# Attention of the third token block spread over five row tiles, its inputs loaded earlier, its decays on GpSimd

## The chip, the cores and the metric

One core of a Trainium2 chip runs the whole program. The metric is the device time of one execution in microseconds (us), as the median of several runs; the profile is one execution of its own, with its own time.

## The reference

Three layers follow one another, all in float32 precision. First a retention (linear attention with decay) over batch 4, 8 heads, 768 positions, head size 64. Then an ELU layer from 512 to 2048 and back, and a "maxout" layer with three 512 x 768 matrices and a last 768 x 512 matrix, on 3072 tokens.

```python
for t in range(S):                        # retention, for each batch and head
    state = gamma * state + outer(k[t], v[t])
    y[t] = scale * q[t] @ state
h = x @ w_in                              # ELU layer
x = where(h > 0, h, exp(min(h, 0)) - 1) @ w_out
h = maximum(maximum(x @ w1, x @ w2), x @ w3)
return h @ w_out2
```

The moe weights are float64 numbers, which the kernel turns into float32 pairs (high and low part) itself.

## The kernel before

**Chunks, blocks, steps.** The 3072 tokens are 24 chunks `c` of 128 tokens (6 to a batch) and 6 blocks `b` of 512 tokens (4 chunks each). Retention is done by chunk: `scores` multiplies k and q (16 small matmuls, L153), `mask` multiplies them by the decay mask on VectorE (L165), `prep` makes the decayed `qd` (L129) and `kd` (L137), `update` adds this chunk to the running state (PE L181, VectorE L188 and L191), `mix` multiplies state and `qd` (L204) and the masked scores and v (L208), and copies the result to `xh` on ScalarE (L216); `rest` makes its low part `xl` on VectorE (L221). `begin(c)` is scores, prep and mask; `end(c)` is update and mix. A block's ELU layer runs over 16 row tiles `f` of the hidden layer: `h1(b, f)` is 12 matmuls (L338), then exp, relu, max, and a split into high part `gh` (ScalarE, L348) and low part `gl` (VectorE, L351); `o1(b, f)` is 12 matmuls (L370) that add to four accumulators in PSUM.

**Order.** `seq` (L492 and below) lists pairs (b, f). Blocks 0 and 1 take turns while their weights are still being converted; they fill steps i = 0 to 31, blocks 2 to 5 follow from step 32 (`split`). Step i of the main loop (L767) issues h1 of entry i+1 and then o1 of entry i. The orders of SyncE's DMA queue, TensorE, VectorE and ScalarE are the order of the program text; GpSimd's is the scheduler's. Steps 26 to 29 are (1, 12) to (1, 15), steps 30 and 31 are (0, 14) and (0, 15), and step 32 is (2, 0). Step 26's o1 begins at 207.66 us of the profile, step 32's at 271.95 us. Chunks 8 to 11 (`EARLY` is 8) are block 2, so their attention has to be done before h1(2, 0), which step 31 issues; chunk 12 begins block 3. In steps 28 to 31 the kernel does this:

```python
if i == split - 6: load(c)                        # c = 8
if i == split - 4: prep(c); scores(c, ...); mask(c)
if i == split - 3: load(c + 1); new_x(2); end(c); rest(c); prep(c + 1)
if i == split - 2: load(c + 2); scores(c + 1, ...); mask(c + 1); end(c + 1)
                   load(c + 3); begin(c + 2); rest(c + 1)
if i == split - 1: o1(b, f, f0, f1); end(c + 2); begin(c + 3); load(c + 4); rest(c + 2)
                   end(c + 3); rest(c + 3); begin(c + 4); x2_out(...); h1(*seq[i + 1][:2])
```

From block 3 on, `values` and `following` spread one chunk over four steps. `x2_out` closes a group of steps: VectorE adds the accumulators to a partial sum, four instructions (L387), and SyncE writes the sums out where the block is done.

**Buffers.** A chunk of block 0 or 1 lies in a slot of `wpool` (13 slots of 8 KB per partition, tag `w`), a later one in `ld` (2 slots, tag `r`, shared with the partial sums of x2_out). A load from chunk 8 on is five DMAs: four of 128 KB (L98), one of 512 KB (L106). A slot of `wpool` otherwise holds the converted weights of one f below 13; those of f = 9 to 12 are written to DRAM (`keep`, `kept`) and fetched again into `ring` (3 slots for each of two halves) for blocks 2 and up (`fetch`, L416). `qd`, `kd` and `a` have one buffer each; odd chunks below 8 use a `spare` slot of `wpool` in their place. Scores, updates, mixes and h1 share the four PSUM buffers of `ps_h`. `xh` and `xl` have two buffers each, which blocks 0 and 1 hold until the h1 of their f = 15, in steps 28 and 30. In steps up to 27 VectorE converts one half of an f per step (L279 to L306) from `raw`, which `load_half` (L243) has SyncE load two halves ahead.

Of the kernel before, what the change touches and what calls it, by code (L numbers as in the profile page):

```python
# [7 lines left out]
F32 = mybir.dt.float32  # L8
# [7 lines left out]
B, H, S, D = 4, 8, 768, 64  # L16
P = 128
# [13 lines left out]
RES = 9  # L31
# [9 lines left out]
def kernel(ctx: ExitStack, tc: tile.TileContext, qkv0, qkv, wa, wb, dmask, qdec, cols, out):  # L41
# [18 lines left out]

    dmask_sb = const.tile([P, H, P], F32, name="dmask_sb")
    qdec_sb = const.tile([P, NPAIR, P], F32, name="qdec_sb")
    cols_sb = const.tile([P, H + NPAIR], F32, name="cols_sb")
    state = [const.tile([P, NPAIR, D], F32, name=f"state{i}") for i in range(2)]
    x2d = dram.tile([KDM, P, NT], F32, name="x2d")
    kept = {(f, c): dram.tile([P, 2 * 512], F32, name=f"kept{f}_{c}") for f in range(RES, KFF) for c in range(2)}
# [11 lines left out]
    def load(c, part=None):  # L78


        if c >= NCHUNK:
            return

        early = c < EARLY
        src = qkv0 if early else qkv
        if part != 1:
            if c in raw_t:
                return
            if early:
                x = wpool.tile([P, NPAIR, 4, P], F32, tag="w", name="x")  # L90
            else:
                x = ld.tile([P, NPAIR, 4, P], F32, tag="r", name="x")
            raw_t[c] = x
            for r in range(2):
                h = slice(r * D, (r + 1) * D)
                for s in range(1 if early else 2):
                    cc = slice(s * 2 * P + r * P, s * 2 * P + (r + 1) * P)
                    nc.sync.dma_start(out=x[h, :, s, :], in_=src[c, :, h, cc].rearrange("p d t -> d p t"))  # L98
            if early:
                nc.sync.dma_start(  # L100
                    out=x[:, :, 1, :], in_=src[c, :, :, 2 * P:3 * P].rearrange("p t n -> t p n")
                )
        if part != 0:
            x = raw_t[c]
            o = 3 * P if early else 4 * P
            nc.sync.dma_start(  # L106
                out=x[:, :, 2:4, :].rearrange("t p s n -> t p (s n)"),
                in_=src[c, :, :, o:].rearrange("p t n -> t p n"),
            )
# [3 lines left out]
    def prep(c):  # L113

        if c >= NCHUNK:
            return
        x = raw_t[c]
        early, pool = c < EARLY, nc.vector if c <= EARLY + CB else nc.gpsimd
        if early and c % 2:
            if not spare:  # L120
                spare.append(wpool.tile([P, 4, NPAIR, P], F32, tag="w", name="spare"))
            sp = spare[0]
            qd, kd, a = sp[:, 0], sp[:, 1].rearrange("t p (r d) -> t p r d", r=2), sp[:, 2:4]
        else:
            qd = at.tile([P, NPAIR, P], F32, tag="qd", name="qd") if c % NCH != 0 else None
            kd = at.tile([P, NPAIR, 2, D], F32, tag="kd", name="kd") if c % NCH != NCH - 1 else None
            a = None
        if c % NCH != 0:
            pool.tensor_tensor(out=qd, in0=x[:, :, 0, :], in1=qdec_sb, op=ALU.mult)  # L129
        kt = x[:, :, 2, :].rearrange("t p (r d) -> t p r d", r=2)  # L130
        if c % NCH == NCH - 1:
            pass
        elif early:
            for h in range(H):
                nc.scalar.activation(kd[:, h // 2, h % 2], kt[:, h // 2, h % 2], ACTF.Copy, scale=cols_sb[:, h:h + 1])
        else:
            pool.tensor_tensor(  # L137
                out=kd, in0=kt,
                in1=cols_sb[:, 0:H].rearrange("t (p r) -> t p r", r=2).unsqueeze(3).to_broadcast([P, NPAIR, 2, D]),
                op=ALU.mult,  # L140
            )
        st_t[c] = (qd, kd, a)

    def scores(c, pool, tag):

        if c >= NCHUNK:
            return
        x = raw_t[c]
        sc = sc_t[c] = [pool.tile([P, NPAIR, P], F32, tag=tag, name="sc") for _ in range(2)]
        for p in range(NPAIR):  # L150
            for r in range(2):
                h = slice(r * D, (r + 1) * D)
                nc.tensor.matmul(sc[r][:, p, :], x[h, p, 1, :], x[h, p, 0, :], start=p == 0, stop=p == NPAIR - 1)  # L153

    def mask(c):
        if c >= NCHUNK:
            return
        sc = sc_t.pop(c)
        a = st_t[c][2]
        if a is None:  # L160
            a = at.tile([P, 2, NPAIR, P], F32, tag="a", name="a")
        else:
            a = a.rearrange("t r p i -> t r p i")
        for r in range(2):
            nc.vector.tensor_tensor(  # L165
                out=a[:, r], in0=sc[r], in1=dmask_sb.rearrange("j (p r) i -> j r p i", r=2)[:, r], op=ALU.mult
            )
        a_t[c] = a
# [358 lines left out]
    def begin(c, pool=ps_h, tag="h"):  # L527
        scores(c, pool, tag)
        prep(c)
        mask(c)  # L530

    def end(c):
        update(c, ps_h, "h")
        mix(c, ps_h, "h")
# [232 lines left out]
    for i, (b, f, f0, f1) in enumerate(seq):  # L767
        if i < 2:
            continue
        if (b, f0) in units:  # L770
            done = (units[b, f0] - 1) * CB + f // CB
            if f % CB == 1:
                values(done)
            elif f % CB == 2:
                following(done)
        c = EARLY
        if i == split - 6:
            load(c)
        if i == split - 4:
            prep(c)  # L780
            scores(c, ps_h, "h")
            mask(c)
        if i == split - 1:
            part_t[b] = []
            for m in range(KDM):
                o = f32(dpool.tile([P, BLK], (I32, F32)[m % 2], tag="tm"[m % 2], name="tm"[m % 2]))
                nc.sync.dma_start(out=o, in_=x2d[m, :, b * BLK:(b + 1) * BLK])
                part_t[b].append(o)
            o1(b, f, f0, f1)
            end(c + 2)  # L790
            begin(c + 3)
            load(c + 4)
            rest(c + 2)
            end(c + 3)
            rest(c + 3)
            begin(c + 4)
            x2_out(b, f0, f1, False)
            h1(*seq[i + 1][:2])
            continue
        if i == len(seq) - 5:  # L800
            pump(100000)
            reopen()
            load_sums(0)
            sums(0)
            for k in XORD:
                later.append(lambda k=k: split_sum(0, k))
        if i == len(seq) - 4:
            fetch_set(loads[-1][0])
        if i == len(seq) - 3:
            fetch_set(loads[-1][1])  # L810
            fetch_set(loads[-1][2])
        if i + 1 == len(seq):
            break
        if i < split and n < 2 * KFF:
            h1(*seq[i + 1][:2], [(cv_high, n)], [(cv_bits, n + 1)] if n + 1 < 2 * KFF else [])
        elif i >= len(seq) - 5:
            h1(*seq[i + 1][:2], [], [(catch_up, 1)])
        elif i > split:
            h1(*seq[i + 1][:2], [(pump, 2)], [(pump, 2)])
        else:  # L820
            h1(*seq[i + 1][:2])
        o1(b, f, f0, f1)
        if f == f1 - 1:
            x2_out(b, f0, f1, f1 < KFF and (b, f0) != (0, 10))
        if i >= len(seq) - 5:
            catch_up(2)
        elif i > split:
            pump(1 if b < NB - 1 and f % CB in (1, 2) else 4)
        if i == split - 3:
            load(c + 1)  # L830
            new_x(2)
            end(c)
            rest(c)
            prep(c + 1)
        if i == split - 2:
            load(c + 2)
            scores(c + 1, ps_h, "h")
            mask(c + 1)
            end(c + 1)
            load(c + 3)  # L840
            begin(c + 2)
            rest(c + 1)
        if i < split and n < 2 * KFF:
            cv_low(n)
            if n + 1 < 2 * KFF:
                cv_rest(n + 1)
            n += 1
            if i == 2:
                cv_high(n)
                cv_bits(n + 1)  # L850
                cv_low(n)
                cv_rest(n + 1)
                n += 1
        while i < split and done_f < n // 2:
            if done_f >= RES:
                keep(done_f)
            done_f += 1
        for c, g in ((0, i + 1), (1, i)):
            if g < len(seq):
                b, f = seq[g][:2]  # L860
                if f >= KFF - NRING and (b + 1 < NB if b >= 2 else (b, f) in ((1, 13), (0, 14), (0, 15)) and g > 24):
                    fetch(RES + f - (KFF - NRING), c)
                if b >= 2 and RES <= f < KFF - NRING:
                    fetch(f + NRING, c)
    catch_up(99)
# [105 lines left out]
```

## Time and profile before

| | |
|---|---|
| median of 3 runs | 1034.04 us (1031.86 to 1034.31) |
| profiled execution: its time, its span | 1032.82 us, 1030.7 us |
| busy: TensorE, VectorE, ScalarE, GpSimd | 98%, 67%, 34%, 2% of the span |
| granted TensorE clock, mean | 0.989 |

The span runs from the first to the last instruction; the 2.1 us beside it lie around the program. The clock is a share of 2.4 GHz. PE is TensorE's matmuls, PEld its weight loads, DVE VectorE, ACT ScalarE, POOL GpSimd, SPq the DMA queue of SyncE. A row of a timeline merges neighbouring instructions of one kind (x16 is sixteen of them), and names in brackets how long the engine was idle before it and what ended that.

### The profile page before, as it was taken

How to read it: one execution, taken by the hardware profiler on the slowest of the kernel's cores; microseconds unless marked ns; L12 is line 12 of the kernel's file. 1: busy time of each engine (PE TensorE's matmuls, PEld its weight loads, DVE VectorE, ACT ScalarE, POOL GpSimd, SP SyncE). 2: the span in 40 equal slices, each digit the busy share in tenths (PEclk: the TensorE clock that was granted, in tenths of full speed). 3: DMA queues.
4: the chain of work that ended last, by engine and by line, in shares of the span. 5: the costliest groups of instructions: out<-in, count | busy, mean ns of one | idle time of the engine just before them, and what ended most of it. 6: DMA issues, size and time to landing. Idle time of an engine off the chain costs nothing.

```text
span 1030.7 us, 14358 instructions
## 1 busy us (share of the span) xinstructions
PE 1005.3 (98%) x5693; PEld 856.9 (83%) x5693; DVE 690.6 (67%) x1197; ACT 353.8 (34%) x629; POOL 23.7 (2%) x23
## 2 busy tenths in 40 slices
PE   7989999998899999999999999999999999999998
PEld 4767888876688887788788788899999989999996
DVE  2879888875466776677766652678748846874771
ACT  3556555531244444444444443511301121130110
POOL 0000000000000100000100000000000000000000
PEclk8999999999899999999999999999999999999999
DMA  9633235579523794388446743996237036303701
GB/s 244 165 93 122 92 128 190 166 273 262 158 82 115 228 331 158 130 279 265 151 152 234 257 183 110 379 358 245 72 136 272 2 115 223 143 11 131 276 2 62
DMA packets 75170, 180.24 MB, mean 175 GB/s; under 512 B 5856, under 2 KB 42720, under 8 KB 70880
## 3 DMA queue, kind: packets, MB, share of 16 engines
q1 hardware_dynamic: 73376, 176.19, 50.7%
q10 hardware_dynamic: 1728, 3.15, 0.8%
q8 instruction: 45, 0.74, 0.3%
q14 instruction: 21, 0.17, 0.1%
HBM read 138.68 MB, written 40.63 MB: 174 GB/s over the span
## 4 chain that ended last, share of the span: by engine, by line
PE 90%; DMA 3%; DVE 3%; ACT 2%; SPq 1%; issue 0%; DVEq 0%; ACTq 0%
PE pp L681 25%; PE hp L338 25%; PE acc L370 23%; PE ac L733 9%; DMA x<-in_qkv 2%; PE xo L208 2%; PE sc L153 2%; PE xo L204 2%; PE up L181 1%; SPq L98 1%; PE junk L525 1%; DMA w<-kept 1%; DVE e L347 0%; DVE part L387 0%; ACT gh L348 0%
## 5 line engine op out<-in xcount | busy, mean ns | idle before, releaser
L681 PE MATMUL pp<-xs,op 128*128 128x384 f32 x1512 | 267.8, 334 | 0.0
L681 PEld LDWEIGHTS pp<-xs,op 128*128 128x128 f32 x1512 | 263.3, 188 | 3.0
L338 PE MATMUL hp<-xh,w 128*128 128x512 f32 x768 | 251.6, 399 | 2.1 <-ACT w L300 2.1
L370 PE MATMUL acc<-gh,w 128*128 128x512 f32 x768 | 196.6, 395 | 2.3 <-DVE part L391 1.7
L338 PEld LDWEIGHTS hp<-xh,w 128*128 128x128 f32 x768 | 144.7, 189 | 37.9 <-ACT w L300 2.5
L370 PEld LDWEIGHTS acc<-gh,w 128*128 128x128 f32 x768 | 143.3, 188 | 37.7 <-issue 2.3
L347 DVE SCALAR_TENSOR_TENSOR e<-e,hp 128x512 f32<-128x512 f32 x96 | 65.9, 686 | 125.3 <-ACT e L346 125.3
L338 PE MATMUL hp<-xl,w 128*128 128x512 f32 x384 | 144.0, 395 | 0.0
L733 PE MATMUL ac<-w,g 128*128 128x512 f32 x432 | 104.5, 391 | 0.0
L370 PE MATMUL acc<-gl,w 128*128 128x512 f32 x384 | 104.3, 393 | 0.0
L345 ACT ACTIVATE e<-hp 128x512 f32<-128x512 f32 x96 | 57.3, 597 | 127.5 <-PE hp L338 127.4
L733 PEld LDWEIGHTS ac<-w,g 128*128 128x128 f32 x432 | 80.6, 188 | 14.9
L348 ACT CAST gh<-e 128x512 fp32r<-128x512 f32 x96 | 59.6, 621 | 86.4 <-DVE e L347 86.4
L697 ACT COPY u<-pp 128x384 f32<-128x384 f32 x36 | 17.3, 479 | 201.5 <-PE pp L681 127.5
L370 PEld LDWEIGHTS acc<-gl,w 128*128 128x128 f32 x384 | 72.1, 188 | 16.6
L338 PEld LDWEIGHTS hp<-xl,w 128*128 128x128 f32 x384 | 72.6, 189 | 15.9
L351 DVE TENSOR_TENSOR gl<-e,gh 128x512 fp32r<-128x512 f32 x96 | 66.2, 690 | 19.8 <-ACT gh L348 16.9
L689 DVE TENSOR_TENSOR c<-pp,u 128x384 f32<-128x384 f32 x96 | 52.9, 553 | 36.1 <-PE pp L681 35.6
L346 ACT ACTIVATE e<-e 128x512 f32<-128x512 f32 x96 | 60.7, 632 | 3.1
L282 ACT ACTIVATE t<-t 128x512 int32<-128x512 int32 x56 | 35.4, 633 | 49.4 <-DVE t L279 49.4
L300 ACT CAST w<-t 128x512 fp32r<-128x512 f32 x56 | 34.8, 621 | 37.9 <-DVE t L297 37.9
L711 DVE TENSOR_TENSOR h<-h,c 128x768 f32<-128x768 f32 x48 | 45.9, 957 | 1.6
(69 smaller groups left out, 824.3 us busy)
## 6 DMA issues: line engine op xcount, KB each, us to landing
op<-opd SPq DMA_DIRECT2D x24, 1792.0 KB, 7.5
w<-kept SPq DMA_DIRECT2D x55, 512.0 KB, 6.3
raw<-in_wa SPq DMA_DIRECT2D x32, 512.0 KB, 3.8
x<-in_qkv SPq DMA_DIRECT2D x24, 512.0 KB, 6.3
raw<-in_wb SPq DMA_DIRECT2D x24, 512.0 KB, 4.2
x<-in_qkv SPq DMA_DIRECT2D x80, 128.0 KB, 4.4
opd<-w SPq DMA_DIRECT2D x9, 1024.0 KB, 7.9
kept<-w SPq DMA_DIRECT2D x14, 512.0 KB, 4.7
```

Source lines behind the costliest of these rows:

```text
L282: nc.scalar.activation(t, t, ACTF.Relu, scale=8.0, bias=-896.0 * 2 ** 23)
L338: nc.tensor.matmul(hp, w[:, pw, kk * P:(kk + 1) * P], x[px][:, kk, :], start=k == 0, stop=k == len(order) - 1,)
L345: nc.scalar.activation(e, hp, ACTF.Exp)
L346: nc.scalar.activation(e, e, ACTF.Relu, scale=-1.0, bias=1.0)
L347: nc.vector.scalar_tensor_tensor(out=e, in0=e, scalar=-1.0, in1=hp, op0=ALU.mult, op1=ALU.max)
L348: nc.scalar.copy(gh, e)
L351: nc.vector.tensor_tensor(out=gl, in0=e, in1=f32(gh), op=ALU.subtract)
L370: nc.tensor.matmul(acc_t[b][m], w[:, p[0], m * P:(m + 1) * P], g[p[1]], start=f == f0 and p == first, stop=f == f1 - 1 and p == final,)
L681: nc.tensor.matmul(o, ws[i][:, pw, kk * P:(kk + 1) * P], xs[i][:, px, kk, :], start=k == 0, stop=k == 5)
L689: nc.vector.tensor_tensor(out=out, in0=a, in1=c, op=ALU.add)
L711: nc.vector.tensor_tensor(out=h_t[s, p][i], in0=h_t[s, p][i], in1=c[i], op=ALU.max)
L733: nc.tensor.matmul(ac_t[s, m], g[:, px, m * P:(m + 1) * P], wo_t[f][:, pw, :], start=first and i == 0, stop=final and i == 2,)
```

## The change

- The attention of chunks 8 to 12 moves from steps 28 to 31 to steps 27 to 32, one chunk to a step: scores and mask of chunk 8 at the head of step 27, of 9 in step 28, 10 in 29, 11 in 30 and 12 in step 32; end and rest of chunks 8 to 11 at the tail of steps 27 to 30. `new_x(2)` moves from step 29 to step 27.
- The loads of chunks 8, 9, 10, 11 and 12 are issued at the ends of steps 21, 24, 25, 27 and 30. Those of 8 to 10 go to slots of `wpool`, which the weights of f = 9 to 12 leave free after their last o1 in blocks 0 and 1 (f = 9 in step 19, 10 in step 22, 11 in step 23, 12 in step 26). Those of 11 and 12 go to `ld`.
- `prep` of chunks 8 to 12 runs on GpSimd instead of VectorE; that of chunk 8 is issued in step 25, of 9 in step 27, 10 in 28, 11 in 29, 12 in 31. Chunks 9 and 11 use a `spare` slot again.
- The six fetches of f = 9 to 11 for block 2 move from steps 26 to 31 to steps 32 to 35. The partial sum of block 0 is read back in step 30 instead of 31.
- The tile of `cols` is 128 bytes wide per partition instead of 48 (the DMA into it is the same), so that the tiles allocated behind it (state, w, raw, r, qd, kd, a, and VectorE's t and m) begin at a multiple of 128 bytes instead of 64 bytes past one.

```diff
-    cols_sb = const.tile([P, H + NPAIR], F32, name="cols_sb")
+    cols_sb = const.tile([P, 32], F32, name="cols_sb")[:, :H + NPAIR]
...
-            if early:
+            if c < EARLY + 3:
                 x = wpool.tile([P, NPAIR, 4, P], F32, tag="w", name="x")
...
-        early, pool = c < EARLY, nc.vector if c <= EARLY + CB else nc.gpsimd
-        if early and c % 2:
-            if not spare:
-                spare.append(wpool.tile([P, 4, NPAIR, P], F32, tag="w", name="spare"))
+        early = c < EARLY
+        pool = nc.vector if early else nc.gpsimd
+        if c < EARLY + CB and c % 2:
+            if c in (1, EARLY + 1):
+                spare[:] = [wpool.tile([P, 4, NPAIR, P], F32, tag="w", name="spare")]
...
-        if i == split - 6:
-            load(c)
-        if i == split - 4:
-            prep(c)
-            scores(c, ps_h, "h")
-            mask(c)
-        if i == split - 1:
+        if split - 5 <= i < split - 1 or i == split:
+            k = c + min(i - split + 5, 4)
+            scores(k, ps_h, "h")
+            mask(k)
+        if i == split - 2:
             part_t[b] = []
...
+        if i == split - 1:
             o1(b, f, f0, f1)
-            end(c + 2)
-            begin(c + 3)
-            load(c + 4)
-            rest(c + 2)
-            end(c + 3)
-            rest(c + 3)
-            begin(c + 4)
             x2_out(b, f0, f1, False)
             h1(*seq[i + 1][:2])
+            prep(c + 4)
             continue
...
-        if i == split - 3:
-            load(c + 1)
...
+        for at_step, k in ((11, c), (8, c + 1), (7, c + 2), (5, c + 3), (2, c + 4)):
+            if i == split - at_step:
+                load(k)
+        if i == split - 7:
+            prep(c)
+        if split - 5 <= i < split - 1:
+            if i == split - 5:
+                new_x(2)
+            end(c + i - split + 5)
+            rest(c + i - split + 5)
+        for at_step, k in ((5, 1), (4, 2), (3, 3)):
+            if i == split - at_step:
+                prep(c + k)
...
-                if f >= KFF - NRING and (b + 1 < NB if b >= 2 else (b, f) in ((1, 13), (0, 14), (0, 15)) and g > 24):
+                if b >= 2 and f >= KFF - NRING and b + 1 < NB:
                     fetch(RES + f - (KFF - NRING), c)
+                if b == 2 and 1 <= f <= NRING:
+                    fetch(RES + f - 1, c)
```

## Rows read from the trace of the kernel before

**Rows 1.** The page, busy time, share of the span and instructions by engine.

```profile
PE 1005.3 (98%) x5693; PEld 856.9 (83%) x5693; DVE 690.6 (67%) x1197; ACT 353.8 (34%) x629; POOL 23.7 (2%) x23
```

**Rows 2.** Busy time by stretch: length, PE, PEld, DVE, ACT, POOL; clock, DMA, GB/s.

```profile
207.66:271.95 64.29, 55.80 (x401) 44.67 (x399) 35.81 (x63) 15.17 (x25) 0.00 (x0) 0.89 0.80 243
...
236.00:246.00 10.00, 8.26 (x86) 6.86 (x85) 5.23 (x9) 1.29 (x3) 0.00 (x0) 0.83 0.94 230
...
262.00:272.00 10.00, 9.43 (x40) 7.44 (x39) 5.04 (x9) 1.85 (x3) 0.00 (x0) 0.69 0.45 143
```

**Rows 3.** Waits from 190 to 285 us: total, times, longest.

```profile
PE sc L153 <- DMA x<-in_qkv: 6.8, 3, 5.7
...
PE up L181 <- DVE kd L137: 1.7, 1, 1.7
```

**Rows 4.** The chain of waits, 185 to 290 us: start, us, what.

```profile
239.95 0.70 DVE kd L137
...
240.75 1.10 PE up L181 x16
...
255.33 7.12 DMA x<-in_qkv
...
264.63 7.40 PE hp L338 x24
```

**Rows 5.** Timeline of SyncE's DMA queue: start, us, issues.

```profile
183.10 4.51 SPq L412 DMA_DIRECT2D kept<-w  x2
...
248.75 0.98 SPq L416 DMA_DIRECT2D w<-kept  x2
...
252.10 3.83 SPq L98 DMA_DIRECT2D x<-in_qkv  x4
```

**Rows 6.** Timeline of TensorE: the starts of five o1.

```profile
279.34 2.03 PE L370 MATMUL acc<-gh,w 128*128 128x512 f32 x8
...
286.23 2.03 PE L370 MATMUL acc<-gh,w 128*128 128x512 f32 x8
...
291.82 2.03 PE L370 MATMUL acc<-gh,w 128*128 128x512 f32 x8
...
297.43 2.03 PE L370 MATMUL acc<-gh,w 128*128 128x512 f32 x8
...
305.72 2.03 PE L370 MATMUL acc<-gh,w 128*128 128x512 f32 x8
```

**Rows 7.** TensorE by stretch: length, busy, granted clock, DMA share, GB/s.

```profile
39.70:43.45 3.75, 3.75 (x66) 1.00 0.78 233
...
249.20:255.50 6.30, 6.30 (x97) 1.00 1.00 338
...
252.00:253.00 1.00, 1.00 (x18) 1.00 1.07 424
```

**Rows 8.** Groups by line: count, busy us, mean ns, idle before, its releasers.

```profile
L129 POOL TENSOR_TENSOR qd<-x,qdec_sb 128x512 f32<-128x512 f32 x10 | 13.6, 1365 | 483.1 <-DMA x<-in_qkv 294.4 <-PE xo L204 165.0 <-DMA raw<-in_wb 23.6
...
L137 POOL TENSOR_TENSOR kd<-x,cols_sb 128x512 f32<-128x512 f32 x9 | 9.9, 1102 | 30.2 <-PE up L181 21.0 <-DMA x<-in_qkv 8.4 <-POOL qd L129 0.6
...
L137 DVE TENSOR_TENSOR kd<-x,cols_sb 128x512 f32<-128x512 f32 x4 | 2.8, 692 | 10.9 <-DMA x<-in_qkv 10.9
```

**Rows 9.** Timeline, GpSimd and VectorE at 301 us; then L290 over the whole span.

```profile
301.55 1.27 POOL L129 TENSOR_TENSOR qd<-x,qdec_sb 128x512 f32<-128x512 f32 x1 [23.85 <-PE xo L204]
301.69 1.68 DVE L290 SCALAR_TENSOR_TENSOR m<-raw,m 128x512 f32<-128x512 uint32 x1
...
L290 DVE SCALAR_TENSOR_TENSOR m<-raw,m x56: 691/693/1683, 33.2 to 605.7; 128x512 f32<-128x512 uint32 x56
```

**Rows 10.** Timeline of VectorE: the end of its conversions for step 26.

```profile
214.96 0.68 DVE L347 SCALAR_TENSOR_TENSOR e<-e,hp 128x512 f32<-128x512 f32 x1
```

**Rows 11.** The start: chain of waits, then busy time by stretch as in rows 2.

```profile
3.84 7.42 DMA x<-in_qkv
...
12.00:16.00 4.00, 2.97 (x27) 2.98 (x29) 0.42 (x1) 2.63 (x9) 0.00 (x0) 0.51 1.16 262
...
20.00:24.00 4.00, 4.00 (x67) 3.36 (x65) 2.27 (x4) 2.02 (x8) 0.00 (x0) 1.00 1.09 354
```

More of the change, by code (lines that the diff above doesn't have):

```diff
@@ L828 @@
             pump(1 if b < NB - 1 and f % CB in (1, 2) else 4)
-        if i == split - 3:
-            load(c + 1)
[L831 to L842, printed above, removed]
+        for at_step, k in ((11, c), (8, c + 1), (7, c + 2), (5, c + 3), (2, c + 4)):
[11 more added lines that the diff above has]
+                prep(c + k)
         if i < split and n < 2 * KFF:
```

## The prediction

> **What bounds the kernel now.** I read the page first: TensorE is busy for 98% of the span and nothing else comes near [rows 1], so time can only be won where TensorE stands still or runs slowly. The busy time by stretch then shows where that is: from step 26's o1 to step 32's, TensorE was busy for 55.80 of 64.29 us, so 8.49 us were idle, at a mean granted clock of 0.89 [rows 2]. The list of waits names what ended that idleness: the scores waited 6.8 us for inputs, once for 5.7, and an update 1.7 us for a decayed k that VectorE could not make before its input had landed [rows 3]. The chain of waits shows the same in order of time: kd at 239.95, the update at 240.75 and the last load, 7.12 us on the chain [rows 4]. Each long wait is followed by a time at 1.2 GHz, half the full clock: 0.83 and 0.69 are the means of the stretches behind them [rows 2]. The sixteen matmuls of an update then take 1.10 us, and two h1 together 7.40 us [rows 4]. Why the inputs are late is on SyncE's queue: the load of chunk 12 begins at 252.10 us, right behind two fetches of 512 KB, and a chunk's slot in `ld` comes free only when the chunk two before it is done [rows 5].
>
> **The change part by part.** *The stretch itself.* The same matmuls are issued in another order, so I build the stretch from undisturbed pitches. A step without attention takes 291.82 - 286.23 = 5.59 us; with scores 286.23 - 279.34 = 6.89, so scores cost 1.30; with L204, L208 and an update 305.72 - 297.43 = 8.29, so these cost 2.69 [rows 6]. From step 26's o1 to step 32's are six steps, 6 x 5.6 = 33.6. Five scores, three full ends and one end without an update (chunk 11 closes a batch; I take 2.1 for it) add 5 x 1.30 + 3 x 2.69 + 2.1 = 16.7. That is 50.3 us; where scores directly follow an end, the step pays its 0.2 us of entry once and not twice, three times, so 49.7. I take 49.9 against 64.29: **-14.4 us**, between -14.0 and -14.8. Idle time and clock come near it: 8.49 us idle; a mean clock of 0.83 over 10 us is 3.4 us at half clock, one of 0.69 is 6.2 [rows 2], and half of these 9.6 is lost, 4.8; together 13.3, without what ran slowly just ahead of 262 us.
>
> *The loads.* They are hidden if they land before the scores. Four issues of L98 took 3.83 us [rows 5]; with the fifth a load is under 5 us of queue and, by the longest chain piece, 7.12 us [rows 4] to land. Chunk 8 has six steps (33 us), chunks 9 to 11 three to four; chunk 12, behind the writes and the read-back of partial sums on the queue, about 10 us, the tightest. The queue passes each load ahead of `raw` halves, but the halves of the conversion are due a whole step (5.6 us) later, and from half 32 on they are due after step 32. The fetches, 3 MB, are due at step 40 and go out from step 32. Cost: nothing; the cover is the TensorE work of the steps between issue and use, and without it a load costs up to 7.12 us each, as now.
>
> *Decays on GpSimd.* VectorE loses eight instructions of 0.69 us, which were off the path but for the one wait above. GpSimd gains four `qd` of 1.365 and four `kd` of 1.102 us [rows 8], each one step ahead of its reader. They are not free for VectorE: while GpSimd made a `qd` for 1.27 us, VectorE's L290 took 1.68 us, against a median of 0.693 [rows 9]. So each such instruction can hold VectorE for about 1 us, 8 in all. In steps 22 to 27 VectorE has little room: it begins e(1, 14) at 214.96, 4.5 us after the start of step 27, still behind with step 26 [rows 10]. The split of an h1 is due two half-steps later (about 7 us), so 2 us more do not show there. The Trainium skill, SBUF — State Buffer, section "SBUF: two separate sides", says why: VectorE and GpSimd share a port pair as an exclusive lock, held for the whole instruction, also against VectorE instructions with two SBUF inputs. The trace agrees: 1.68 us against 0.693 [rows 9].
>
> *A new wait.* `new_x(2)` in step 27 needs the buffers of block 1, whose last reader is h1(1, 15) in step 28. So ScalarE's copy xh(8) stands from the end of mix(8) until that h1 is done, about 4 us (1.1 of scores, 2.8 of h1). Behind it on ScalarE is only the exp of that same h1; on VectorE `rest(8)` and behind it the last conversion, mask(9) and e(1, 15). TensorE meanwhile needs PSUM: xo(8) keeps one of four `ps_h` buffers until `rest(8)`, two go to scores(9), one to h1(1, 15); the last comes free with VectorE's state update of chunk 8. Followed on like this, buffer and need meet within 0.1 us in steps 28 to 30 (an h1 waits for the `up` buffer of the chunk before), and a GpSimd instruction that holds VectorE just there, qd(11) in step 29 is the one I expect, makes TensorE wait 0.8 us. Lower bound 0; upper bound all of a GpSimd pair at three places, 3 x (1.365 + 1.102) = 7.4. I take **+1.0**, because two of three places have no GpSimd work at the same time.
>
> *The wider constants.* No row shows the effect of where a tile begins. Upper bound of a gain: the start waits 7.42 us for chunk 0, while 262 GB/s move; at the 354 GB/s of the stretch from 20 us on it would be 7.42 x (1 - 262/354) = 1.9 us less [rows 11]. Lower bound: nothing, since 424 GB/s went into tiles behind `cols` in longer runs, and these begin 64 bytes off as well [rows 7]. A loss has no reason. Nearest to nothing: **-0.4**. The Trainium skill, DMA: Bandwidth & Descriptors, section "How a descriptor splits into AXI transactions", would put a 512-byte piece that starts 64 bytes before a 256-byte boundary at 22 beats and an aligned one at 16. No row here shows it; if it holds for writes, my estimate from it is 7.42 x 6/22 = 2.0 us at the start, and the sum would be 1017.4.
>
> **Sum**, against the profiled execution's own time: 1032.82 - 14.4 + 1.0 - 0.4 = **1019.0 us**. That execution lies 1.2 us under the median of 1034.04 and inside the runs shown.
>
> **The rivals.** *VectorE gives half of it back.* If the GpSimd pairs meet the tight buffers in all three steps, 7.4 replaces 1.0: 1025.4. For it: rows 9, and the chain of buffers. Against: after step 27 VectorE has no conversion left, some 4 us of work in steps of 9. Held in full by all eight, 4 x 1.365 + 4 x 1.102 = 9.9 us, and all of it on TensorE's path, the time would be 1032.82 - 14.4 - 0.4 + 9.9 = 1027.9. This is what the exclusive lock of the Trainium skill (SBUF — State Buffer, same section) would cost at most. Chance 10 in 100.
>
> *The small matmuls cost the clock.* Three steps now have 2.69 + 1.30 us of small matmuls between two full runs. If the clock fell after each as after the wait at 239 us, 3.4 us at half clock, 1.7 lost each time: 1019.0 + 5.1 = 1024.1. Against: the same pieces in the same order had clock 1.00 from 39.70 to 43.45, and 6.30 us of them from 249.20 too [rows 7]. What preceded both falls was idleness. Chance 4.
>
> *The loads stay late.* If chunk 11's or 12's slot in `ld` is freed late after all, one wait of 5.7 us [rows 3] and its slow stretch (6.2 us at half clock, 3.1 lost) stay: 1019.0 + 8.8 = 1027.8. Chance 4.
>
> *Slower: a load stands at the head of SyncE's queue.* Load(8) goes out at about 183 us [rows 5], in step 21, and everything behind it waits with it, the `raw` halves first. If its slot is not that of f = 9 (last read in step 19, seven pitches before 207.66, about 168 us) but one read until step 26 (o1 done at 210.4), the queue stands 27 us; the next half is due some 11 us after it would be issued, so TensorE loses about 16 to 20, the net is 2 to 6 slower, about 1036. It decides at a stand of some 25 us. Against: four slots come free and four are asked for, each in order. Chance 5.
>
> **Chances and range.** The forecast has 77 in 100. Its own range is 1016.1 (-14.8, nothing for the waits, -1.9) to 1021.8 (-14.0, 3 us of waits, nothing for the constants). To leave out no more than 2 in 10, I go to the middle of the rivals: 1015.5 to 1025.5. A measurement of this kernel tells about 0.3%, 3.1 us, from no change. Faster by more than that: the forecast and most of the first three, 0.92; within it 0.03; slower 0.05.
>
> **What would show it.** Right: from step 26's o1 to step 32's about 51 us, no wait of scores for x, the clock at 1.00 throughout, `x` issued from about 183 us on, eight more GpSimd instructions before 275 us, and no change of any length behind step 33. Wrong: waits of h1 or scores on VectorE's state or rest of more than 1 us in steps 28 to 30; waits of L243 on TensorE on SyncE's queue around 183 to 210; a clock under 1.00 there; VectorE conversions late enough that an o1 waits for its weights in steps 23 to 27.

## The result and the profile after

The changed kernel takes 1018.55 us in the median of four runs (1018.1 to 1019.52), against 1033.59 us for the kernel before on the same chip: a ratio of 0.9858, interval 0.9845 to 0.9871 (ratios are taken over the runs, so they differ a little from those of the medians). The forecast was 1019.0 us. The profiled execution took 1019.52 us, its span is 1017.7 us, 13.0 less than before.

The page, busy time by engine, answers to [rows 1]; GpSimd has eight more instructions, as forecast:

```profile
PE 999.9 (98%) x5690; PEld 853.6 (84%) x5693; DVE 690.5 (68%) x1189; ACT 353.3 (35%) x629; POOL 33.9 (3%) x31
```

Busy time by stretch, from step 26's o1 to step 32's (columns as in [rows 2]), then two lines of the list of waits in it:

```profile
207.68:259.93 52.25, 49.95 (x401) 39.88 (x400) 34.63 (x54) 15.12 (x25) 7.76 (x6) 1.00 0.70 227
```

```profile
ACT xh L217 <- PE hp L339: 5.1, 1, 5.1
PE hp L339 <- DVE state L192: 2.3, 3, 1.3
```

The stretch is 12.04 us shorter than in [rows 2], at full clock, and no matmul waits for an input any more, against 6.8 us in [rows 3]. What is idle now is 2.30 us, all of it h1 waiting for VectorE's state update. The timeline of TensorE has the three places, in steps 28, 29 and 30:

```profile
222.44 1.17 PE L339 MATMUL hp<-xh,w 128*128 128x512 f32 x4 [1.29 <-DVE state L192]
...
232.69 0.50 PE L339 MATMUL hp<-xh,w 128*128 128x512 f32 x1 [0.77 <-DVE state L192]
...
242.45 0.50 PE L339 MATMUL hp<-xh,w 128*128 128x512 f32 x1 [0.24 <-DVE state L192]
```

The timelines of GpSimd and VectorE ahead of these places:

```profile
210.78 1.27 POOL L130 TENSOR_TENSOR spare<-x,qdec_sb 128x512 f32<-128x512 f32 x1 [17.35 <-DMA x2d<-part]
212.00 1.50 POOL L138 TENSOR_TENSOR spare<-x,cols_sb 128x512 f32<-128x512 f32 x1
218.16 1.04 POOL L138 TENSOR_TENSOR kd<-x,cols_sb 128x512 f32<-128x512 f32 x1 [4.66 <-PE up L182]
219.16 1.72 POOL L130 TENSOR_TENSOR qd<-x,qdec_sb 128x512 f32<-128x512 f32 x1
229.95 1.27 POOL L130 TENSOR_TENSOR spare<-x,qdec_sb 128x512 f32<-128x512 f32 x1 [9.07 <-PE xo L205]
```

```profile
211.15 1.44 DVE L298 SCALAR_TENSOR_TENSOR t<-raw,t 128x512 int32<-128x512 int32 x1
212.52 1.53 DVE L352 TENSOR_TENSOR gl<-e,gh 128x512 fp32r<-128x512 f32 x1
...
218.22 1.53 DVE L298 SCALAR_TENSOR_TENSOR t<-raw,t 128x512 int32<-128x512 int32 x1
219.67 1.76 DVE L352 TENSOR_TENSOR gl<-e,gh 128x512 fp32r<-128x512 f32 x1
...
221.87 0.42 DVE L192 TENSOR_TENSOR state<-up,state 128x256 f32<-128x256 f32 x1
...
230.33 1.44 DVE L352 TENSOR_TENSOR gl<-e,gh 128x512 fp32r<-128x512 f32 x1 [0.69 <-ACT gh L349]
...
239.06 2.48 DVE L388 TENSOR_TENSOR part<-acc,part 128x512 f32<-128x512 f32 x4
...
241.97 0.42 DVE L192 TENSOR_TENSOR state<-up,state 128x256 f32<-128x256 f32 x1
```

Four VectorE instructions that take 0.69 us alone took 6.26 together while GpSimd made the decays of chunks 9 and 10: 3.5 us held. The state comes at 222.29, and h1 starts 0.15 us later. Ahead of the second wait one instruction takes 1.44 us beside GpSimd's qd of chunk 11. Ahead of the third GpSimd does nothing: there the state stands behind the four adds of `x2_out` in VectorE's own queue.

The rest of the 13.0 us: up to 207.68 nothing (207.66 before), and 0.96 from step 32's o1 on. The first load in the queue's timeline stands at 183.11 us, as forecast, 27.5 us ahead of its scores at 210.57 (33 were forecast); chunk 12's goes out at 244.02, 12 us ahead of its scores at 255.96:

```profile
183.11 2.58 SPq L98 DMA_DIRECT2D x<-in_qkv  x4
...
244.02 2.58 SPq L98 DMA_DIRECT2D x<-in_qkv  x4
```

### The profile page after: what moved, and what is told of

It reads as the page before. It is cut to its first block, busy times and chain, and to the rows that moved or that the text cites. A ratio compares the mean times of both kernels' runs of the same rounds, so it can differ in the third digit from the quotient of the medians.

```text
span 1017.7 us, 14387 instructions
## 1 busy us (share of the span) xinstructions
PE 999.9 (98%) x5690; PEld 853.6 (84%) x5693; DVE 690.5 (68%) x1189; ACT 353.3 (35%) x629; POOL 33.9 (3%) x31
## 4 chain that ended last, share of the span: by engine, by line
PE 91%; DVE 5%; ACT 2%; DMA 1%; issue 1%; SPq 0%; DVEq 0%; ACTq 0%
PE pp L682 26%; PE hp L339 25%; PE acc L371 24%; PE ac L734 9%; PE xo L209 2%; PE sc L154 2%; PE xo L205 2%; PE up L182 1%; DVE gl L352 1%; DVE e L348 1%; DMA x<-in_qkv 1%; PE junk L526 1%; DVE t L298 1%; ACT gh L349 0%; DVE part L388 0%
## 5 line engine op out<-in xcount | busy, mean ns | idle before, releaser
L352 DVE TENSOR_TENSOR gl<-e,gh 128x512 fp32r<-128x512 f32 x96 | 68.8, 717 | 19.6 <-ACT gh L349 16.9
```

Source lines behind the costliest of these rows:

```text
L352: nc.vector.tensor_tensor(out=gl, in0=e, in1=f32(gh), op=ALU.subtract)
```

## The experiments

All of them compute everything, and each was measured beside the kernel before on its own chip (that kernel's medians there are 1032.7 to 1033.6 us), so the ratios compare better than the medians. Each has one profile. "Stretch" is from the start of step 26's o1 to step 32's in the profile, idle is TensorE's in it; before it is 64.29 and 8.49 us, after 52.25 and 2.30.

| kernel | median us | ratio to before, interval | stretch, idle |
|---|---|---|---|
| changed kernel | 1018.55 | 0.9858 (0.9845 to 0.9871) | 52.25, 2.30 |
| 1 changed, narrow cols | 1020.24 | 0.9880 (0.9866 to 0.9893) | 52.18, 2.30 |
| 2 before, wide cols | 1029.93 | 0.9973 (0.9964 to 0.9982) | 62.51, 7.68 |
| 3 changed, decays on VectorE | 1018.06 | 0.9857 (0.9843 to 0.9870) | 51.32, 1.40 |
| 4 before, early loads and late fetches | 1018.50 | 0.9864 (0.9849 to 0.9879) | 49.94, 0 |
| 5 before, early loads alone | 1018.57 | 0.9855 (0.9835 to 0.9875) | 49.94, 0 |
| 6 as 4, wide cols | 1017.42 | 0.9843 (0.9822 to 0.9864) | 49.94, 0 |
| 7 changed, fetches back | 1017.03 | 0.9838 (0.9821 to 0.9855) | 51.16, 1.34 |
| 8 changed, loads late | 1047.91 | 1.0131 (1.0108 to 1.0155) | 82.21, 21.57 |
| 9 changed, loads one step ahead | 1028.74 | 0.9957 (0.9946 to 0.9969) | 61.79, 8.31 |
| 10 changed, state first | 1016.21 | 0.9828 (0.9810 to 0.9845) | 49.78, 0.03 |
| 11 as 10, load(7) earlier | 1017.52 | 0.9845 (0.9824 to 0.9865) | 49.76, 0.02 |

**4 to 6: the transfers without the new order.** The kernel before with the loads at their new places, old order of attention, decays on VectorE; in 4 and 6 with the fetches moved too, in 6 with the wide cols. The loads of chunks 8 to 10 go to slots of `wpool`, as in the changed kernel; those at the old places are gone. Two pieces of the edit:

```diff
-            if early:
+            if c < EARLY + 3:
                 x = wpool.tile([P, NPAIR, 4, P], F32, tag="w", name="x")
...
+        for at_step, k in ((11, c), (8, c + 1), (7, c + 2), (5, c + 3), (2, c + 4)):
+            if i == split - at_step:
+                load(k)
```

> The kernel before (order of attention, decays on VectorE, 48-byte cols) with only the loads of chunks 8 to 12 and the fetches at the places of the changed kernel. Theory: the inputs were the larger part; the waits for x (6.8 us) and the 5 us at half clock behind them go, but steps 30 and 31 still hold three chunks back to back, so scores, mask, mix and update wait for VectorE: 1022 to 1026 us, with 3 to 6 us of waits on VectorE. Rival A (transfers are all): 1019 to 1020. Rival B (the order is what counts, the waits only change their names): 1030 or more.

> The kernel before with the loads alone at the places of the changed kernel; the fetches stay in steps 26 to 31. Theory: with the loads ahead of them the fetches delay nothing but load(12), which has 10 us: 1018.5 us, stretch 50 us. Rival (the fetches on the queue were half of the cause): a wait of scores(12) or (11) of 2 to 5 us with a stretch at half clock: 1022 us or more.

> The kernel before with the loads and fetches at the places of the changed kernel and the 128-byte tile of cols, but the old order of attention and the decays on VectorE. Theory (the order and GpSimd bring nothing, they cost 2.3 us of waits for the state): stretch 49.9 us without a wait, steps 33 to 94 in 379.7 us instead of 380.3, so 2 us under the changed kernel: 1016.5 us. Rival (the narrow run with the old order was lucky): 1018.5 us, with waits on VectorE in steps 30 and 31.

Busy time by stretch of 4, then of 5, from step 26's o1 to step 32's:

```profile
207.15:257.09 49.94, 49.94 (x402) 40.03 (x400) 35.65 (x63) 15.17 (x25) 0.00 (x0) 1.00 0.66 212
```

```profile
208.06:258.00 49.94, 49.94 (x401) 40.04 (x399) 35.65 (x63) 15.17 (x25) 0.00 (x0) 1.00 0.80 264
```

TensorE is busy for all of it. My theory of 3 to 6 us on VectorE falls, rival A comes nearest: in this stretch the early loads, with the slots that let them go out early, are the whole gain, the fetches none of it (49.94 in both). The spreading and GpSimd add 2.3 us to this stretch. That 6 is faster than the changed kernel (1016.5 expected, 1017.42 measured) the intervals don't settle.

**8 and 9: how early.** The changed kernel with the loads of chunks 8 to 11 at the ends of steps 26 to 29, so directly ahead of their scores in the program (8), or at the heads of these steps (9); chunk 12 as it is, and `prep(8)` one step later in both. The edit of 8:

```diff
-        for at_step, k in ((11, c), (8, c + 1), (7, c + 2), (5, c + 3), (2, c + 4)):
+        for at_step, k in ((6, c), (5, c + 1), (4, c + 2), (3, c + 3), (2, c + 4)):
...
-        if i == split - 7:
+        if i == split - 6:
             prep(c)
```

> The changed kernel with each load of chunks 8 to 11 one step ahead of its scores (ends of steps 26 to 29) instead of two to six; chunk 12 as it is. Theory: a load needs about 5 us of queue and landing, and a step with attention is 9.5 us, so most is hidden; chunks 8 and 9 follow a step of 5.6 us and 9 us and meet raw and kept on the queue, so scores(8) wait 0 to 2 us: 1018.5 to 1021. Rival (the lead of two to six steps is what brings the gain): each of four loads shows 3 to 5 us and the clock falls: 1028 or more.

> The changed kernel with the loads of chunks 8 to 11 at the head of the step before their scores (heads of steps 26 to 29), where the late loads stood at its end. Theory: what made the late loads slow is the place on SyncE's queue, behind raw and kept, which wait for VectorE; at the head of the step they are ahead of that step's raw and kept and have 5.6 to 9.5 us, so scores(8) wait 1 to 3 us, the others under 1: 1019 to 1023 us. Rival (a lead of one step is too little whatever the place): four waits of 3 to 5 us and a lower clock: 1035 or more.

In 8 the rival holds, and it is 14 us slower than the kernel before. In 8, the waits of SyncE's queue, then the three longest of TensorE (chunks 8, 9 and 11), then VectorE's longest waits:

```profile
SPq L244 <- DVE t L298: 23.2, 4, 13.4
SPq L413 <- DVE w L307: 14.4, 3, 12.8
SPq L394 <- DVE part L388: 13.4, 6, 11.2
```

```profile
218.12 0.76 PE L154 MATMUL sc<-x 64*128 64x128 f32 x2 [7.84 <-DMA x<-in_qkv]
...
236.90 2.44 PE L154 MATMUL sc<-x 64*128 64x128 f32 x16 [5.51 <-DMA x<-in_qkv]
...
267.23 0.76 PE L154 MATMUL sc<-x 64*128 64x128 f32 x2 [4.67 <-DMA x<-in_qkv]
```

```profile
DVE e L348 <- ACT e L347: 17.4, 5, 5.3
DVE xl L222 <- ACT xh L217: 16.1, 2, 14.1
DVE a L166 <- PE sc L154: 7.8, 2, 6.0
```

I had counted 5 us for queue and landing and left out that the queue itself stands. Load(8) goes out at 211.93 us, when TensorE has stood since 210.28. Load(9) stands behind a `raw` that waits 13.4 us for VectorE's conversion (L298), and VectorE has stood for the late scores(8) and the h1 behind them (6.0 and 5.3 us); load(10) stands behind a `kept`, and VectorE at `rest(8)` for 14.1 us; load(11) stands behind the writes of the partial sums. So each late load makes the next one late. In 9 neither forecast holds: only chunks 8 and 10 wait (the two pairs of waits are 5.65 and 2.41 us), chunks 9 and 11 are there in time; the queue waits 8.3 us for L307 once, ahead of load(10):

```profile
209.87 3.81 SPq L98 DMA_DIRECT2D x<-in_qkv  x4
...
226.47 9.08 SPq L413 DMA_DIRECT2D kept<-w  x2
235.64 2.64 SPq L98 DMA_DIRECT2D x<-in_qkv  x4
```

So place on the queue and lead both count. The step of lead that chunk 8 has in the program was 0.6 us on the chip: load(8) goes out at 209.87, behind writes of partial sums and a `kept` that wait for VectorE, and TensorE is ready for scores(8) at 210.46.

**3: the decays on VectorE.** Only the engine of `prep` for chunks 8 to 12 changes.

```diff
-        pool = nc.vector if early else nc.gpsimd
+        pool = nc.vector if c <= EARLY + CB else nc.gpsimd
```

> The changed kernel with the decays of chunks 8 to 12 on VectorE, at the same places in the program. Theory: GpSimd's instructions hold VectorE for about a us each and cause the three waits of h1 for the state (2.3 us); but in VectorE's own queue prep(9) stands behind rest(8), which waits for xh(8), so kd(9) comes 1.4 us after it and mask(9) later still; the update of chunk 9 then waits about 1 us, and two of the three waits go. Net between 1 us faster and 1 us slower: 1017.5 to 1019.6. Rival (the port does not matter, only the instruction count): VectorE has 5.5 us more to do in a stretch of 52, hidden: 1018.6 with the same three waits.

As expected, two of the three waits go and one of 1.02 us comes, though at the mix of chunk 9, on its mask, and not at its update. The timeline of TensorE in 3 has the new one and the one that stays, which is that behind the adds of `x2_out`:

```profile
227.38 1.09 PE L205 MATMUL xo<-spare,state 64*64 64x128 f32 x16 [1.02 <-DVE spare L166]
240.48 0.50 PE L339 MATMUL hp<-xh,w 128*128 128x512 f32 x1 [0.23 <-DVE state L192]
```

The two kernels can't be told apart by their times: GpSimd brings nothing here. In the stretch 0.9 of the 2.3 us go without it (52.25 to 51.32).

**10 and 7: the waits for the state.** In 10 the decays of chunks 10 and 11 go to VectorE, where it stands idle, and the update of chunk 10 ahead of the adds of x2_out (pieces of the edit):

```diff
-        pool = nc.vector if early else nc.gpsimd
+        pool = nc.vector if early or c in (EARLY + 2, EARLY + 3) else nc.gpsimd
...
+        if i == split - 3:
+            update(c + 2, ps_h, "h")
         if f == f1 - 1:
             x2_out(b, f0, f1, f1 < KFF and (b, f0) != (0, 10))
...
+            mix(k, ps_h, "h")
+            if k == c:
+                prep(c + 2)
+            rest(k)
```

> The changed kernel with the decays of chunks 10 and 11 on VectorE at places where it stands idle (qd and kd of 10 between the state of chunk 8 and rest(8), qd of 11 behind mask(10)), and in step 29 the update of chunk 10 ahead of the four adds of x2_out. Theory: GpSimd no longer runs while the states of chunks 8 and 9 are due, and that of chunk 10 comes 2.4 us sooner, so the three waits of h1 for the state (1.29, 0.77, 0.24 us) go: 1016.3 us, stretch 50 us. Rival (the waits come from the number of PSUM buffers alone): they stay within 0.5 us of what they are: 1018 to 1018.6.

The busy time of 10 by stretch, from step 26's o1 to step 32's:

```profile
207.33:257.11 49.78, 49.75 (x402) 39.89 (x401) 33.88 (x57) 15.11 (x25) 3.78 (x3) 1.00 0.75 243
```

The waits are gone, and the median is 1016.21 (1016.3 expected), the lowest of all, though its interval overlaps those of 3, 5, 6, 7 and 11. Which of the two changes removed which wait, 10 alone does not show. In 7 only the fetches are back at steps 26 to 31.

> The changed kernel with the six fetches of f = 9 to 11 back in steps 26 to 31. Theory: with the loads issued steps ahead the fetches delay nothing that is due; load(12) lands behind three of them, some 3 us later, which its 6 us of margin hold: 1018.6, no wait for x in the stretch. Rival (3 MB in the stretch crowd out the loads): a wait of scores(12) of 3 us or more: 1021 or more.

No wait for x, as expected; but the first wait for the state went too, which I had not foreseen. In its timelines GpSimd makes the decays of chunk 9 from 220.55 on instead of 210.78, and L298 and L352 take the 0.69 us that they take alone:

```profile
218.32 1.04 POOL L138 TENSOR_TENSOR kd<-x,cols_sb 128x512 f32<-128x512 f32 x1 [26.05 <-PE xo L205]
219.32 1.27 POOL L130 TENSOR_TENSOR qd<-x,qdec_sb 128x512 f32<-128x512 f32 x1
220.55 1.29 POOL L130 TENSOR_TENSOR spare<-x,qdec_sb 128x512 f32<-128x512 f32 x1
```

```profile
216.04 0.68 DVE L298 SCALAR_TENSOR_TENSOR t<-raw,t 128x512 int32<-128x512 int32 x1
216.81 0.69 DVE L352 TENSOR_TENSOR gl<-e,gh 128x512 fp32r<-128x512 f32 x1
217.42 0.42 DVE L189 TENSOR_TENSOR state<-state,cols_sb 128x256 f32<-128x256 f32 x1
```

So the first wait hangs on when GpSimd runs, not on how much it does: it still makes six decays in the stretch. The second wait stays, 1.10 us, and the third, 0.24.

**1, 2 and 11: the wide cols and the start.**

```diff
-    cols_sb = const.tile([P, 32], F32, name="cols_sb")[:, :H + NPAIR]
+    cols_sb = const.tile([P, H + NPAIR], F32, name="cols_sb")
```

> The changed kernel with the 48-byte tile of cols. Theory: the 128-byte tile gave nothing lasting at the start (chunk 0 about 1.3 us earlier, lost again by 62 us to a stretch at half clock), but 0.8 us from step 33 to step 91, in the steps whose weights lie in the slots behind cols, about 0.02 us each. So the narrow tile costs 0.8: about 1019.4 us, the first update back at 13.0 us instead of 12.0, and the stretch of steps 26 to 32 unchanged at 52.2 us. Rival: the drift has another cause (the fetches, or where the weights lie by chance); then 1018.6 us.

> The kernel before with only the 128-byte tile of cols. Theory: the same 0.8 us, and faster landings of x (320 against 250 GB/s in the first 30 us) that shorten the waits of steps 28 to 31 by 1 to 2 us: 1031 to 1032 us. Rival (nothing from the constants): 1033.6 us.

Kernel 2 is 0.27% or 2.8 us faster than before, more than expected; its profile has 1.8 of it in the stretch and 0.6 in steps 33 to 94. Kernel 1 is 0.0022 above the changed kernel in ratio, 2.3 us, but the intervals overlap a little. Its profile shows the 0.7 of steps 33 to 94 (380.29 us against 379.60, between the starts of their o1) and an equal stretch; the remaining us or so I can't place, since its profiled execution is the fastest of its four.

The 0.7 us lies in the steps whose weights are in slots behind cols. In block 5, the starts of h1 for f = 2, 9, 10 and 15, before and then after:

```profile
585.06 0.40 PE L338 MATMUL hp<-xh,w 128*128 128x512 f32 x1
...
624.26 0.40 PE L338 MATMUL hp<-xh,w 128*128 128x512 f32 x1
...
629.81 0.39 PE L338 MATMUL hp<-xh,w 128*128 128x512 f32 x1
...
657.04 0.39 PE L338 MATMUL hp<-xh,w 128*128 128x512 f32 x1
```

```profile
572.31 0.40 PE L339 MATMUL hp<-xh,w 128*128 128x512 f32 x1
...
611.34 0.39 PE L339 MATMUL hp<-xh,w 128*128 128x512 f32 x1
...
616.86 0.40 PE L339 MATMUL hp<-xh,w 128*128 128x512 f32 x1
...
644.09 0.39 PE L339 MATMUL hp<-xh,w 128*128 128x512 f32 x1
```

Seven steps with resident weights take 39.20 and 39.03 us; five with weights from the ring, which lies ahead of cols in both kernels, 27.23 and 27.23. Kernel 1, which differs from the changed kernel in cols alone, has 39.20 and 27.23 too. But of the nine profiles with wide cols only seven have 39.03 to 39.05; 9 has 39.12 and 3 has 39.20, as the four narrow ones do. So wide cols go with the gain, and why it is missing in block 5 of 3 is open; in blocks 3 and 4 all nine have it. Kernel 11 moves `load(7)` directly behind `load(6)` in the program.

> The version with the state first (prep of 10 and 11 on VectorE, update of 10 ahead of the adds), and load(7) directly behind load(6) in the first 40 us. Theory: the 1.2 us that the faster landing of x wins at the start are lost at 54 to 62 us, where scores(7) and its update wait for x and kd of chunk 7 (1.16 and 1.27 us) and the clock falls; with chunk 7 there these go and the gain stays: 1 to 2.5 us faster, 1014 to 1015 us. Rival (VectorE is full from 42 to 62 us and sets the pace): 1016.2 us.

Nothing is won (1017.52 us), as the rival has it: the wait for x of chunk 7 is gone, and the update waits 1.94 us for kd on ScalarE instead of 1.27. VectorE, which the rival names, is busy for 16.75 of the 20 us from 42 to 62; that it sets the pace there is not shown.

## Why the prediction was right, step by step

- **The stretch, -14.4.** Confirmed for TensorE's work: without waits it is 49.94 (4 to 6) and 49.78 us (10), against 49.9 worked out from pitches. In the changed kernel it is 49.95 busy and 2.30 idle, 52.25 where about 51 was named as the sign of being right.
- **The loads cost nothing.** Confirmed, and more: they alone are the gain. The cover I named is real, since without it (8) three waits alone cost 18.0 us and the mean clock of the stretch falls to 0.83. The prediction did not split the 14.4 us between the loads and the new order; 4 and 5 show that the order has no part in them.
- **VectorE and GpSimd, the new wait, +1.0.** The mechanism was right, PSUM held until a state update that GpSimd delays; the term was mis-sized, 2.30 us. I placed one hit, of 0.8 us in step 29 (measured 0.77). Wrong was that the other places have no GpSimd work at the same time: ahead of step 28's h1 the pairs of chunks 9 and 10 together hold VectorE 3.5 us, and that h1 waits 1.29 us. A wait of more than 1 us there was one of my own signs of being wrong. The third wait, 0.24 us, is the adds of `x2_out`; it stays in 3, where GpSimd does nothing in the stretch. The copy xh(8) stood 5.1 us for h1(1, 15), 4 expected; nothing on TensorE waited for it. The rule of the Trainium skill on the shared port (SBUF — State Buffer, section "SBUF: two separate sides") agrees with the stretched instructions above, 1.44 to 1.76 us instead of 0.69.
- **The constants, -0.4.** Right in sign, wrong in place. At the start the stretch from 12 to 16 us moves 317 GB/s instead of 262, 297 in kernel 2 and 263 in kernel 1; over all thirteen profiles it is 297 to 322 with wide cols and 255 to 263 with narrow ones. That chunk 0 lands earlier, 6.34 us on the chain after its last issue instead of 7.42 [rows 11], is not shown to come from cols: it takes 5.96 to 7.71 us in the wide profiles and 6.93 to 7.77 in the narrow ones. The reason for the lower bound was misread as well: most of what moved at 424 GB/s [rows 7] were, by the size of the packets (0.41 of 0.42 MB in rows of 4096 bytes), the two fetches issued at 248.75 [rows 5], into `ring`, which lies ahead of `cols`. And by 62 us the changed kernel's lead of 1.3 us is gone: TensorE waits for kd of chunk 7 and runs the next matmuls slowly:

```profile
57.09 2.15 PE L182 MATMUL up<-x,spare 128*64 128x64 f32 x16 [1.27 <-ACT spare L136]
59.17 1.97 PE L205 MATMUL xo<-spare,state 64*64 64x128 f32 x16
```

  "No change of any length behind step 33" was wrong by 0.8 us, in the steps with resident weights.
- **The sum.** 14.4 and 1.0 became 14.3 (64.29 - 49.95) and 2.3; the constants gave 0.8 behind step 33 instead of 0.4 at the start. The profiled execution lost 13.3 us (1032.82 to 1019.52), 13.8 forecast. That the sum is within 0.5 us is in part luck: the waits were 1.3 larger, and against them stand 0.6 more behind step 32 and 0.3 outside the span, which was no term of mine.
- **The rivals.** VectorE gave back 2.3 of the 7.4 us allowed. The clock stayed at 1.00 through the small matmuls. Late loads, and a queue that stands, are what 8 made real: slower than before. There the queue stands at `raw`, `kept` and the partial sums and not, as the rival had it, at a load without a slot.

## What to carry to other kernels

Before reordering work around a wait, move only the transfer and look: here five loads issued two to six steps earlier, three of them into free slots, gave all of the stretch's gain, and the new order with GpSimd cost 2.3 us. Where the loads go on an in-order queue counts as much as how early: look at what the instruction ahead of them waits for. And give an idle engine work only at times when the busy one has nothing due that the two can't do at once.

## What the runs showed that I had not expected

- Where the tiles begin bears on what it costs to move and to read them: 255 to 263 GB/s against 297 to 322 in the same four microseconds, and 380.3 to 380.4 us against 379.6 to 379.8 for steps 33 to 94, in the four profiles with narrow cols and the nine with wide ones. In block 5 it is 0.024 us (0.17 over seven) per step of 24 matmuls whose weights begin 64 bytes past a multiple of 128, with the two exceptions above. The Trainium skill, DMA: Bandwidth & Descriptors, section "How a descriptor splits into AXI transactions", would by an estimate have 22 beats against 16 for the short pieces, a factor of 1.38; the stretch shows 1.21 (317 against 262), with other transfers among them. That this rule is the cause no run shows.
- What comes ahead of step 26, nearly the same work in all kernels, ended between 206.6 and 208.8 us in the thirteen profiles, so a difference of 1 us between two spans says nothing by itself; the stretch has to be compared.
